# Where operands begin in SBUF: pools of an attention and feed-forward kernel laid out by role

## The chip, the cores and the metric

The kernel runs on one core of a Trainium2 chip. The metric is the device time of one execution in microseconds (us), the median of the runs shown. Matrix products run on TensorE (PE, with its weight loads as PEld), elementwise work on VectorE (DVE) and ScalarE (ACT), and transfers are issued by SyncE (SP) and GpSimd (POOL).

## The reference

Chunked local attention feeds a two-layer network with a PReLU between the layers. Cut to what matters:

```python
# q, k, v: (8, 8, 576, 64); chunks of 64
scores = scale * q_c @ k_c.T               # per chunk
attn = softmax(scores)
out = attn @ v_c
x = out.transpose(0, 2, 1, 3).reshape(4608, 512)
h = x @ w_in                               # (4608, 512) @ (512, 2048)
g = maximum(h, 0) + alpha * minimum(h, 0)
return g @ w_out                           # (4608, 2048) @ (2048, 512)
```

## The kernel before

The 4608 tokens are 9 blocks of 512 (`TB`). Blocks 0 to 2 are computed plainly ("plain blocks"). Blocks 3 to 8 are taken as three pairs with a fast scheme of seven products instead of eight for 2x2 blocks of each layer (`first_product`, `second_product`). Every float32 operand of the feed-forward part is held as two float32r halves, high and low, and each product is three passes: high by high, high by low, low by high.

All feed-forward matmuls have one shape. The weights (`lhsT`, the stationary operand) are 128x128, the moving operand (`rhs`) is 128x512, and the moving operand is read through `woven`, which goes over a 2048-byte row in four rounds: in each it takes 16 bytes of every 64 bytes in turn. There are 16 chunks `f` of the hidden dimension. In a plain block and chunk, `first_layer` has 12 matmuls with weights from `wi[f]` and the moving operand `xh` or `xl`; `ffn_out` has 12 with weights from the activations `gh`, `gl` and the moving operand `wo[f]`. In a pair, weights are units of 128x2x2x256 that `stream` brings back from DRAM into a ring of four tiles (twice the name "raw", and the rooms of `wi15` and `wo15`); `weight` hands out a half of a unit and, when a unit is used up, drops it and issues the next transfer. The moving operands of a pair's first layer are the seven combinations `ops[i, k]` made by `convert`, which lie in rooms of weight chunks that are dead by then (`rooms`); those of its second layer are made by `operand` in small buffers ("gh", "gl", "g", "ta", "tb", "more", "ob"). The activations `g[f]` of a pair lie in rooms of weight chunks too.

Buffers come from pools. A pool has one place for each name (or `bufs` places), and pools lie behind one another in SBUF in the order in which they are opened. Before the change every `wi`, `wo` chunk and everything put into their rooms is in the one pool `const`. In the kernel before, the whole of `const`, `load`, `soft`, `xp`, `gp` and `stage` has places whose byte address is a multiple of 512, since `small`, ahead of them, ends at byte 5120 and every place is 2048, 4096 or 8192 bytes long; in all the feed-forward matmuls, weights and moving operand both begin at a multiple of 512 bytes.

The order of the start is written out by hand in `START`. After it the order of instructions on an engine comes from a scheduler with priorities, except that PE's matmuls keep program order from step 20 on. Of the steps, PE is fed by `prepare` (splitting weights on DVE and ACT, line 189 writes the low half), by `prelu` and the split behind it (lines 386, 389, 415, 418), and in pairs by lines 703 to 720 and 644, 645. Between steps, `visit` does the attention of later tokens (lines 252 and 368).

Of the kernel before, what the change touches and what calls it, by code (L numbers as in the profile page):

```python
# [59 lines left out]
def tile_local_attention_prelu_ffn(  # L60
# [13 lines left out]
    P = 128  # L74
# [18 lines left out]


    small = ctx.enter_context(tc.tile_pool(name="small", bufs=1))
    const = ctx.enter_context(tc.tile_pool(name="const", bufs=1))
    load = ctx.enter_context(tc.tile_pool(name="load", bufs=1))
    soft = ctx.enter_context(tc.tile_pool(name="soft", bufs=1))
    xp = ctx.enter_context(tc.tile_pool(name="xp", bufs=2))
    gp = ctx.enter_context(tc.tile_pool(name="gp", bufs=2))  # L100
    stage = ctx.enter_context(tc.tile_pool(name="stage", bufs=2))
    dram = ctx.enter_context(tc.tile_pool(name="dram", bufs=1, space=bass.MemoryType.DRAM))
# [12 lines left out]

    def room(n, shape, dtype=F32):
        side, f = ("wi", NF - 1 - n // 2) if n % 2 else ("wo", NF - 1 - n // 2)
        return const.tile(shape, dtype, name=f"{side}{f}")  # L120

    FREE = 12
    RAWS = 6
# [5 lines left out]
    nc.scalar.activation(table, table, AF.Exp)  # L129

    small.tile([P, 24], F32, name="rest")
    ident = small.tile([P, P], F32, name="ident")
    make_identity(nc, ident)
    alpha_sb = small.tile([P, NF], F32, name="alpha_sb")
# [14 lines left out]
    def fetch(side, f):  # L149
        n = fetched[0]  # L150
        fetched[0] += 1
        at = n % (4 + RAWS)
        if n < LISTED and at >= 4:
            raws[side, f] = room(FREE + at - 4, [P, 512], I64)
        else:
            name = ("raw", "raw", "more", "more")[at] if n < LISTED else ("raw", "raw", "more")[(n - 14) % 3]
            raws[side, f] = stage.tile([P, 512], I64, name=name, bufs=2)
        latest[0] = nc.sync.dma_start(out=raws[side, f], in_=(w_in if side == "wi" else w_out)[:, f])

    def piece(side, f, alone=False):  # L160

        raw = raws.pop((side, f))
        words = raw.bitcast(U32).rearrange("p (n two) -> p two n", two=2)
        low, high = words[:, 0], words[:, 1]
        name = HALVES.get(f"{side}{f}", halves_free[0])
        halves_free.remove(name)
        t1 = stage.tile([P, 512], U32, name=name, bufs=1)
        w = const.tile([P, 2, 512], F32R, name=f"{side}{f}")
        (wi if side == "wi" else wo)[f] = w
        hi, lo = w[:, 0], w[:, 1]  # L170
        if alone:
            nc.vector.tensor_scalar(t1, high, 0x7FFFFFFF, None, op0=ALU.bitwise_and)
        else:
            nc.scalar.activation(f32(t1), f32(high), AF.Abs)
        yield
        nc.vector.tensor_scalar(f32(t1), f32(t1), bits(0x38000000), bits(0x47EFFFFF), op0=ALU.max, op1=ALU.min)
        yield
        nc.vector.tensor_scalar(t1, t1, 3, 0x3FFFFFF8, op0=ALU.logical_shift_left, op1=ALU.bitwise_and)
        yield
        nc.vector.scalar_tensor_tensor(t1, in0=high, scalar=0xC0000000, in1=t1, op0=ALU.bitwise_and, op1=ALU.bitwise_or)  # L180
        yield
        nc.vector.scalar_tensor_tensor(t1, in0=low, scalar=29, in1=t1, op0=ALU.logical_shift_right, op1=ALU.bitwise_or)
        yield
        if alone:
            nc.vector.tensor_copy(hi, f32(t1))
        else:
            nc.scalar.copy(hi, f32(t1))
        yield
        split_ends[side, f] = nc.vector.tensor_tensor(lo, f32(t1), f32(hi), op=ALU.subtract)
        halves_free.append(name)  # L190
        yield
# [254 lines left out]
    def store(acc, b, keep, tiles=range(SPB)):  # L446
        for t in tiles:
            o = acc[t]
            rows = slice(b * TB + t * P, b * TB + (t + 1) * P)
            before = partial.get((b, t))  # L450
            if b == PLAIN - 1:
                ob = const.tile([P, DM], F32, name=f"wi{NF - 2 - t}")
            elif keep and b == 0:
                side = "wi" if t % 2 else "wo"
                ob = const.tile([P, DM], F32, name=f"{side}{NF - 1 - t // 2}")
            elif keep:
                pool, name = ((load, "q_sb"), (load, "v_sb"), (load, "v_sb"), (soft, "pr"))[t]
                ob = pool.tile([P, DM], F32, name=name, bufs=1 if name == "pr" else 2)
            elif t < 2:
                if t == 0:  # L460
                    both = stage.tile([P, 2, DM], F32, name="more", bufs=2)
                ob = both[:, t]
            elif t == 2:
                ob = stage.tile([P, DM], F32, name="ob", bufs=1)
            else:
                ob = gp.tile([P, DM], F32, name="g")
            with tc.high_priority(offset=HIGH):
                if b == 1 and t > 1 and not keep:
                    nc.vector.tensor_copy(ob, o)
                else:  # L470
                    nc.scalar.copy(ob, o)  # L471
            if keep:
                partial[b, t] = dram.tile([P, DM], F32, name=f"partial{b}_{t}")
                nc.sync.dma_start(out=partial[b, t], in_=ob)
            elif before is not None:
                if t < 3:
                    adds.append((before, ob))
                else:
                    nc.gpsimd.dma_start(out=before, in_=ob, accum_op=ALU.add)
                finals.append((out[rows, :], before))  # L480
            else:
                nc.sync.dma_start(out=out[rows, :], in_=ob)
# [94 lines left out]
    def combine(side, j, early):  # L577

        ws = wi if side == "wi" else wo
        pair = [ws[j], ws[JF + j]]  # L580
        left, right = halves
        a = []
        for w, name in zip(pair, ("ta", "tb")):
            t = stage.tile([P, 512], F32, name=name, bufs=1)
            nc.vector.tensor_tensor(t, f32(w[:, 0]), f32(w[:, 1]), op=ALU.add)
            a.append(t)
        a11, a22 = a[0][:, left], a[1][:, right]
        if side == "wi":
            a12, a21 = a[0][:, right], a[1][:, left]
        else:  # L590
            a21, a12 = a[0][:, right], a[1][:, left]
        nc.vector.tensor_tensor(a22, a21, a22, op=ALU.add)
        nc.vector.tensor_tensor(a21, a11, a21, op=ALU.subtract)
        nc.vector.tensor_tensor(a11, a22, a11, op=ALU.subtract)
        nc.vector.tensor_tensor(a12, a12, a11, op=ALU.subtract)
        names = ((2, 4), (3, 1)) if side == "wi" else ((2, 3), (4, 1))
        for t, name in zip(a, names):
            which = ("raw", "raw", "more")[(fetched[0] - 14) % 3] if early else ("raw", "more")[fetched[0] % 2]
            fetched[0] += 1
            w = stage.tile([P, 2, 512], F32R, name=which, bufs=2)  # L600
            nc.scalar.copy(w[:, 0], t)
            nc.vector.tensor_tensor(w[:, 1], t, f32(w[:, 0]), op=ALU.subtract)
            for half, s in zip((left, right), name):
                stored = keep_a(side, {1: 5, 2: 6, 3: 7, 4: 3}[s], j, w[:, :, half])
            if adds:
                to, what = adds.pop(0)
                with tc.issue_after(stored.ins):
                    nc.gpsimd.dma_start(out=to, in_=what, accum_op=ALU.add)
# [7 lines left out]
    def stream():  # L616
        at = loaded[0]
        if at == len(sequence):
            return
        loaded[0] += 1  # L620
        if at % RING < 2:
            t = stage.tile([P, 2, 2, 2 * P], F32R, name="raw")
        else:
            t = const.tile([P, 2, 2, 2 * P], F32R, name=("wi", "wo")[at % RING - 2] + str(NF - 1))
        side, n = sequence[at]
        streamed[0] = nc.gpsimd.dma_start(out=f32(t), in_=units[side][n])  # L626
        ring.append((side, n, t))
# [10 lines left out]
        assert ring[0][:2] == (side, n)  # L638
        return ring[0][2][:, u]

    rooms = [f"{side}{f}" for f in range(NF - 1) for side in ("wi", "wo")]

    def split(t, t_hi, t_lo):
        hi = nc.scalar.copy(t_hi, t)  # L644
# [2 lines left out]
    def convert(b):  # L647
# [4 lines left out]
        def step(i, k, t):  # L652
            if (i, 0) not in ops:
                for kk in range(2):
                    ops[i, kk] = const.tile([P, 2, TB], F32R, name=rooms[2 * ORDERS["wi"].index(i) + kk])
            split(t, ops[i, k][:, 0], ops[i, k][:, 1])

        def difference(i, k):
# [8 lines left out]
                return b12  # L667
            return {1: b11, 3: b22, 2: b21}[i]

        order = [(i, k) for i in (1, 2, 7, 5, 6, 3, 4) for k in range(2)]  # L670
        return ops, [lambda i=i, k=k: step(i, k, difference(i, k)) for i, k in order]

    banks = ["ps_h", "ps_h", "ps_o0", "ps_o1", "ps_o2", "ps_o3"]
# [19 lines left out]
    def first_product(ops, g, j):  # L693
# [16 lines left out]
            nc.vector.tensor_tensor(u, e, u, op=ALU.add)  # L710
            nc.vector.tensor_tensor(t, t, u, op=ALU.add)  # L711
        for n, f in enumerate((j, JF + j)):
            g[f] = const.tile([P, 2, TB], F32, name=rooms[14 + 2 * j + n])
        with tc.high_priority(offset=HIGH):
            prelu(g[JF + j][:, 1], t, JF + j)
        for ps, i, f, col in ((c, 3, j, 1), (d, 4, JF + j, 0)):
# [298 lines left out]
```

## Time and profile before

| what | us |
|---|---|
| median of 3 runs | 789.27 (788.91 to 790.05) |
| the profiled execution's own time | 788.34 |
| its span, first to last instruction | 786.6 |
| PE busy | 776.5 (99%) |
| PEld busy | 641.1 (82%) |
| DVE busy | 651.3 (83%) |
| ACT busy | 451.0 (57%) |
| POOL busy | 185.0 (24%) |

A matmul is shown with its whole passage through the pipeline, 0.38 to 0.40 us, and successive ones overlap, so PE's busy time says only that it had work. What a matmul costs in a row of them is the distance from its start to the next one's start. The chain of waits gives that directly: a piece is a row of matmuls with its length, counted from the start of its first to the start of what follows, and their number. Between two answers of the timeline for one engine, of which one ends later, the difference of lengths over the difference of counts is the same distance.

### The profile page before, as it was taken

Reading aid. Unit: us, or ns where it says so; the run is one execution under the profiler, and the core shown is the slowest. Engines: PE = TensorE matmul, PEld = TensorE weight load, DVE = VectorE, ACT = ScalarE, POOL = GpSimd, SP = SyncE. Lnnn points to the kernel's source line nnn. Section 1 sums busy time; section 2 is a strip of 40 time slices with the busy share of each in tenths; the row PEclk is TensorE's granted clock in tenths of the full one; section 3 lists DMA queues with packets and bytes.
Section 4 is the critical chain, followed back from the end, with each engine's and each line's share of the span. In section 5 each row is a group of like instructions: output and inputs, shape, how many; then the busy total and the mean of one; then the engine's idle time right before and its main releaser. Section 6 shows DMA issues by size and latency. Waiting matters only on the chain.

```text
span 786.6 us, 15439 instructions
## 1 busy us (share of the span) xinstructions
PE 776.5 (99%) x5558; PEld 641.1 (82%) x5558; DVE 651.3 (83%) x1140; ACT 451.0 (57%) x1221; POOL 185.0 (24%) x304
## 2 busy tenths in 40 slices
PE   7999999999999999999999999999999999999998
PEld 6788888888878888888888888888888888888886
DVE  6999989997989986777799797777897976678774
ACT  6975555656667565656657456564574444344542
POOL 1153323442424421111112111111112111221110
PEclk9999999999999999999999999999999999999999
DMA  9769495566969776878865778865556765555574
GB/s 359 313 217 370 179 314 203 201 225 182 275 198 276 244 252 206 284 260 268 273 208 193 241 230 296 263 234 184 198 196 220 240 220 199 198 187 190 200 243 143
DMA packets 69323, 184.53 MB, mean 235 GB/s; under 512 B 10992, under 2 KB 18176, under 8 KB 69120
## 3 DMA queue, kind: packets, MB, share of 16 engines
q0 software_dynamic: 34336, 119.56, 44.5%
q1 hardware_dynamic: 34480, 63.20, 23.3%
q8 instruction: 44, 0.72, 0.4%
q10 hardware_dynamic: 432, 0.79, 0.3%
q14 instruction: 31, 0.25, 0.1%
HBM read 135.27 MB, written 42.99 MB: 227 GB/s over the span
## 4 chain that ended last, share of the span: by engine, by line
PE 94%; ACT 2%; DMA 2%; DVE 1%; SPq 1%; issue 0%; ACTq 0%
PE ps_o L688 19%; PE ps_o L805 19%; PE ps_h L401 16%; PE ps_h L805 10%; PE ps_h L688 9%; PE ps_oa L437 8%; PE ps_ob L437 8%; PE ps_a L368 2%; PE ps_a L252 2%; DMA q_sb<-qT 1%; ACT wo L293 1%; ACT wi L293 1%; SPq L318 1%; DMA pT<-t 0%; PE ps_h L853 0%; DMA k_sb<-kT 0%
## 5 line engine op out<-in xcount | busy, mean ns | idle before, releaser
L401 PE MATMUL ps_h<-xh,wi 128*128 128x512 f32 x384 | 102.9, 388 | 0.2 <-ACT xh L353 0.2
L401 PEld LDWEIGHTS ps_h<-xh,wi 128*128 128x128 f32 x384 | 70.9, 187 | 14.1 <-ACT xh L353 0.4
L267 ACT ACTIVATE pr<-ps_a,mx 128x64 f32<-128x64 f32 x224 | 67.7, 329 | 0.9
L688 PE MATMUL ps_o<-wi,raw 128*128 128x512 f32 x168 | 65.5, 390 | 0.0
L688 PE MATMUL ps_o<-wo,raw 128*128 128x512 f32 x168 | 64.9, 387 | 0.0
L644 ACT CAST gh<-wi 128x512 fp32r<-128x512 f32 x57 | 35.5, 623 | 46.9 <-PE ps_o L805 28.2
L437 PE MATMUL ps_oa<-wo,gh 128*128 128x512 f32 x192 | 58.9, 387 | 0.0
L437 PE MATMUL ps_ob<-wo,gh 128*128 128x512 f32 x192 | 58.7, 386 | 0.0
L401 PE MATMUL ps_h<-xl,wi 128*128 128x512 f32 x192 | 51.3, 385 | 0.0
L267 ACT ACTIVATION_READ_ACCUMULATOR pr<-ps_a,mx 128x1 f32 x224 | 49.3, 220 | 0.0
L415 ACT CAST gh<-g 128x512 fp32r<-128x512 f32 x48 | 30.3, 630 | 33.1 <-DVE g L389 25.5
L645 DVE TENSOR_TENSOR gl<-wi,gh 128x512 fp32r<-128x512 f32 x54 | 37.1, 687 | 10.9 <-ACT gh L644 10.7
L626 POOL DMA_DIRECT2D raw<-wi_a x42 | 22.4, 532 | 100.8 <-PE ps_o L688 55.9
L386 ACT ACTIVATE wo<-gh 128x512 f32<-128x512 f32 x24 | 15.2, 632 | 53.5 <-DVE gh L711 53.5
L626 POOL DMA_DIRECT2D raw<-wo_a x42 | 22.3, 531 | 93.6 <-PE ps_o L805 52.5
L401 PEld LDWEIGHTS ps_h<-xl,wi 128*128 128x128 f32 x192 | 35.9, 187 | 7.3 <-DVE xl L355 0.3
L437 PEld LDWEIGHTS ps_ob<-wo,gh 128*128 128x128 f32 x192 | 36.0, 187 | 6.8
L437 PEld LDWEIGHTS ps_oa<-wo,gh 128*128 128x128 f32 x192 | 35.4, 187 | 7.5 <-ACT more L471 0.3
L389 DVE SCALAR_TENSOR_TENSOR g<-g,rise,ps_h 128x512 f32<-128x512 f32 x48 | 35.6, 741 | 2.3 <-ACT g L386 2.2
L437 PE MATMUL ps_oa<-wo,gl 128*128 128x512 f32 x96 | 37.0, 385 | 0.0
L437 PE MATMUL ps_ob<-wo,gl 128*128 128x512 f32 x96 | 36.9, 385 | 0.0
L688 PEld LDWEIGHTS ps_o<-wi,raw 128*128 128x128 f32 x168 | 31.5, 188 | 6.7
(314 smaller groups left out, 2230.0 us busy)
## 6 DMA issues: line engine op xcount, KB each, us to landing
raw<-wi_a POOLq DMA_DIRECT2D x42, 512.0 KB, 4.6
raw<-wo_a POOLq DMA_DIRECT2D x42, 512.0 KB, 3.5
wi<-wi_a POOLq DMA_DIRECT2D x21, 512.0 KB, 4.1
wo<-wi_a POOLq DMA_DIRECT2D x21, 512.0 KB, 4.2
wi<-wo_a POOLq DMA_DIRECT2D x21, 512.0 KB, 3.5
wo<-wo_a POOLq DMA_DIRECT2D x21, 512.0 KB, 3.6
k_sb<-kT SPq DMA_DIRECT2D x28, 256.0 KB, 4.6
q_sb<-qT SPq DMA_DIRECT2D x28, 256.0 KB, 4.0
```

What stands on the lines that cost most here:

```text
L252: pe(nc.tensor.matmul(att[0][c * C:(c + 1) * C, par, (NP + hp) * C:(NP + hp + 1) * C], lhsT=q_sb[rows, 2 * hp + c], rhs=kb[rows, 2 * hp + ...
L267: last = nc.scalar.activation(pr[:, g], sc3[:, g // NP, g % NP], AF.Exp, bias=mx[:, g], scale=SCALE, accum_out=sm[:, g])
L293: last = nc.scalar.activation(pr[:, g], sc3[:, g % 2, g // 2], AF.Exp, bias=mx[:, g], scale=SCALE, accum_out=sm[:, g])
L389: nc.vector.scalar_tensor_tensor(g, in0=g, scalar=rise[:, f:f + 1], in1=h, op0=ALU.mult, op1=ALU.add)
L401: pe(nc.tensor.matmul(woven(hps), lhsT=wi[f][:, l, k * P:(k + 1) * P], rhs=woven(xx[:, k]), start=(i == 0 and k == 0), stop=(i == 2 and k ...
L415: nc.scalar.copy(gh, g)
L437: pe(nc.tensor.matmul(woven(o), lhsT=a[:, ts], rhs=woven(wo[f][:, l]), start=(f == first and i == 0), stop=(f == last and i == 2),))
L626: streamed[0] = nc.gpsimd.dma_start(out=f32(t), in_=units[side][n])
L644: hi = nc.scalar.copy(t_hi, t)
L645: return hi, nc.vector.tensor_tensor(t_lo, t, f32(t_hi), op=ALU.subtract)
L688: pe(nc.tensor.matmul(woven(ps), lhsT=w[:, l, k * P:(k + 1) * P], rhs=woven(xx[:, xl]), start=first and at == 0, stop=at == n - 1, skip_gr ...
L805: pe(nc.tensor.matmul(woven(ps[m]), lhsT=w[:, l, m * P:(m + 1) * P], rhs=woven(xx), start=i in (1, 5, 2) and j == 0 and n == 0, stop=j == ...
```

## The change

The pool `const` is split, and the pools are opened in the order `small`, `ring`, `wo`, `xp`, `gap`, `wi`, `load`, `soft`, `gp`, `stage`. The name "raw" moves from `stage` into `ring`. The chunk `wo15` is made 128 bytes longer and its weights begin behind these; `wi15` is made 64 bytes longer likewise; both chunks lie first in their pools, so that all other chunks of a pool follow at 128 or 64 bytes modulo 512. A tile of 384 bytes, `between`, fills `gap`. The units of the ring that lie in the rooms of `wi15` and `wo15` begin at the start of the place. The moving operands of a pair's first layer go to `wi0` to `wi13`, in the order in which they are converted; a pair's activations go to `wo0` to `wo13`, `wi14` and `wo14`; the results of plain block 2 are staged in `wo14` to `wo11` instead of `wi14` to `wi11`. No instruction is written anew or left out.

```diff
     small = ctx.enter_context(tc.tile_pool(name="small", bufs=1))
-    const = ctx.enter_context(tc.tile_pool(name="const", bufs=1))
+    ring_pool = ctx.enter_context(tc.tile_pool(name="ring", bufs=2))
+    wo_pool = ctx.enter_context(tc.tile_pool(name="wo", bufs=1))
+    xp = ctx.enter_context(tc.tile_pool(name="xp", bufs=2))
+    gap = ctx.enter_context(tc.tile_pool(name="gap", bufs=1))
+    wi_pool = ctx.enter_context(tc.tile_pool(name="wi", bufs=1))
     load = ctx.enter_context(tc.tile_pool(name="load", bufs=1))
     soft = ctx.enter_context(tc.tile_pool(name="soft", bufs=1))
-    xp = ctx.enter_context(tc.tile_pool(name="xp", bufs=2))
...
+    SHIFT = 16
+    sides = {"wi": (wi_pool, 1), "wo": (wo_pool, 2)}
+
+    def place(name, shape, dtype):
+        return sides[name[:2]][0].tile(shape, dtype, name=name)
+
+    def chunk(side, f):
+
+        pool, shifts = sides[side]
+        n = shifts * SHIFT if f == NF - 1 else 0
+        t = pool.tile([P, n + 2 * 512], F32R, name=f"{side}{f}")
+        return t[:, n:].rearrange("p (l n) -> p l n", l=2)
...
+    def scratch(name, shape, dtype):
+        return (ring_pool if name == "raw" else stage).tile(shape, dtype, name=name, bufs=2)
...
+    gap.tile([P, 6 * SHIFT], F32, name="between")
...
-        w = const.tile([P, 2, 512], F32R, name=f"{side}{f}")
+        w = chunk(side, f)
...
-                ob = const.tile([P, DM], F32, name=f"wi{NF - 2 - t}")
+                ob = place(f"wo{NF - 2 - t}", [P, DM], F32)
...
-            t = stage.tile([P, 2, 2, 2 * P], F32R, name="raw")
+            t = scratch("raw", [P, 2, 2, 2 * P], F32R)
         else:
-            t = const.tile([P, 2, 2, 2 * P], F32R, name=("wi", "wo")[at % RING - 2] + str(NF - 1))
+            t = place(("wi", "wo")[at % RING - 2] + str(NF - 1), [P, 2, 2, 2 * P], F32R)
...
-    rooms = [f"{side}{f}" for f in range(NF - 1) for side in ("wi", "wo")]
+    CONVERTED = (1, 2, 7, 5, 6, 3, 4)
+    rooms = [f"wo{f}" for f in range(NF - 2)] + [f"{side}{NF - 2}" for side in ("wi", "wo")]
...
-                    ops[i, kk] = const.tile([P, 2, TB], F32R, name=rooms[2 * ORDERS["wi"].index(i) + kk])
+                    ops[i, kk] = place(f"wi{2 * CONVERTED.index(i) + kk}", [P, 2, TB], F32R)
...
-            g[f] = const.tile([P, 2, TB], F32, name=rooms[14 + 2 * j + n])
+            g[f] = place(rooms[2 * j + n], [P, 2, TB], F32)
```

## Rows read from the trace of the kernel before

**Rows 1.** Page, busy time: engine, us, share of the span, instructions.

```profile
PE 776.5 (99%) x5558; PEld 641.1 (82%) x5558; DVE 651.3 (83%) x1140; ACT 451.0 (57%) x1221; POOL 185.0 (24%) x304
```

**Rows 2.** Waits of PE, the longest: tile and line, engine waited for, us, times, longest.

```profile
PE ps_ob L329 <- ACT wo L293: 1.2, 1, 1.2
PE ps_h L853 <- DVE table L128: 1.1, 1, 1.1
```

**Rows 3.** Chain of waits, in order: start us, length us, engine, tile, line, count.

```profile
76.60 2.68 PE ps_h L401 x12
79.28 1.33 PE ps_oa L437 x6
80.61 1.35 PE ps_ob L437 x6
...
426.06 10.72 PE ps_h L805 x48
436.78 32.15 PE ps_o L805 x144
...
717.59 10.87 PE ps_h L805 x48
728.46 32.66 PE ps_o L805 x144
761.12 10.88 PE ps_h L805 x48
```

**Rows 4.** Windows of lines 401, 437, 688, 805 over the whole span, in this order.

```profile
0.00:786.60 786.60, 139.19 (x576) 106.77 (x576) 1.00 0.69 235
...
0.00:786.60 786.60, 138.19 (x576) 107.33 (x576) 1.00 0.69 235
...
0.00:786.60 786.60, 232.65 (x1008) 187.79 (x1008) 1.00 0.69 235
...
0.00:786.60 786.60, 228.17 (x1008) 188.86 (x1008) 1.00 0.69 235
```

**Rows 5.** PE's timeline around 732 us: start, length, line, out<-in, shape, count.

```profile
731.03 0.38 PE L805 MATMUL ps_o<-gh,raw 128*128 128x512 f32 x1
731.25 0.38 PE L805 MATMUL ps_o<-gl,raw 128*128 128x512 f32 x1
731.48 0.63 PE L805 MATMUL ps_o<-gh,raw 128*128 128x512 f32 x2
731.95 0.39 PE L805 MATMUL ps_o<-gl,raw 128*128 128x512 f32 x1
```

**Rows 6.** PEld's timeline: two loads after a stall, then the same place as above.

```profile
150.35 0.30 PEld L401 LDWEIGHTS ps_h<-xh,wi 128*128 128x128 f32 x2
...
731.03 0.19 PEld L805 LDWEIGHTS ps_o<-gl,raw 128*128 128x128 f32 x1
731.26 0.41 PEld L805 LDWEIGHTS ps_o<-gh,raw 128*128 128x128 f32 x2
```

**Rows 7.** PE's timeline at the start, to 2.5 us and to 4 us.

```profile
1.06 1.86 PE L853 MATMUL ps_h<-wo 128*128 128x128 f32 x7 [1.06 <-DVE table L128]
...
1.06 3.35 PE L853 MATMUL ps_h<-wo 128*128 128x128 f32 x14 [1.06 <-DVE table L128]
```

**Rows 8.** Windows: us, PE, PEld, DVE, ACT, POOL busy (x), PEclk, DMA, GB/s.

```profile
40.00:60.00 20.00, 20.00 (x120) 16.55 (x119) 19.97 (x38) 14.54 (x26) 11.13 (x15) 1.00 0.66 234
60.00:80.00 20.00, 20.00 (x91) 16.75 (x90) 19.49 (x38) 11.47 (x20) 6.80 (x9) 1.00 0.97 368
80.00:100.00 20.00, 20.00 (x91) 16.77 (x90) 18.71 (x35) 11.37 (x20) 5.43 (x8) 1.00 0.47 167
100.00:120.00 20.00, 20.00 (x92) 16.75 (x91) 17.32 (x33) 10.89 (x20) 5.54 (x8) 1.00 0.93 329
```

**Rows 9.** DVE's timeline (split of `wi8`) and PE's timeline (its first use).

```profile
83.75 0.69 DVE L189 TENSOR_TENSOR wi<-tb,wi 128x512 fp32r<-128x512 f32 x1 [0.35 <-ACT wi L187]
...
87.16 0.83 PE L401 MATMUL ps_h<-xh,wi 128*128 128x512 f32 x3
```

**Rows 10.** DMA issues of the ring: count, KB, median us to landing.

```profile
raw<-wi_a POOLq DMA_DIRECT2D x42, 512.0 KB, 4.6
wo<-wi_a POOLq DMA_DIRECT2D x21, 512.0 KB, 4.2
```

**Rows 11.** Costliest DVE group in the pairs: busy us, mean ns, idle before.

```profile
L645 DVE TENSOR_TENSOR gl<-wi,gh 128x512 fp32r<-128x512 f32 x54 | 37.1, 687 | 10.9 <-ACT gh L644 10.7
```

**Rows 12.** Chain of waits between first and second product of the first pair.

```profile
397.35 0.60 DVE gl L645
397.95 0.26 DVE wi L741
398.21 0.27 issue
398.48 0.69 DVE tb L645
399.17 0.04 issue
399.21 26.85 PE ps_o L805 x119
```

More of the change, by code (lines that the diff above doesn't have):

```diff
@@ L113, in woven @@
         return t.rearrange("p (a n c) -> p n a c", n=4, c=4)
+    SHIFT = 16
[7 more added lines that the diff above has]
+        return t[:, n:].rearrange("p (l n) -> p l n", l=2)
     def room(n, shape, dtype=F32):
-        side, f = ("wi", NF - 1 - n // 2) if n % 2 else ("wo", NF - 1 - n // 2)
-        return const.tile(shape, dtype, name=f"{side}{f}")
+        f = NF - 1 - n // 2
+        return place(f"wi{f}" if n % 2 else f"wo{f}", shape, dtype)
+    def scratch(name, shape, dtype):
+        return (ring_pool if name == "raw" else stage).tile(shape, dtype, name=name, bufs=2)
     FREE = 12
@@ L156, in fetch @@
             name = ("raw", "raw", "more", "more")[at] if n < LISTED else ("raw", "raw", "more")[(n - 14) % 3]
-            raws[side, f] = stage.tile([P, 512], I64, name=name, bufs=2)
+            raws[side, f] = scratch(name, [P, 512], I64)
         latest[0] = nc.sync.dma_start(out=raws[side, f], in_=(w_in if side == "wi" else w_out)[:, f])
@@ L451, in store @@
             if b == PLAIN - 1:
-                ob = const.tile([P, DM], F32, name=f"wi{NF - 2 - t}")
+                ob = place(f"wo{NF - 2 - t}", [P, DM], F32)
             elif keep and b == 0:
                 side = "wi" if t % 2 else "wo"
-                ob = const.tile([P, DM], F32, name=f"{side}{NF - 1 - t // 2}")
+                ob = place(f"{side}{NF - 1 - t // 2}", [P, DM], F32)
             elif keep:
@@ L599, in combine @@
             fetched[0] += 1
-            w = stage.tile([P, 2, 512], F32R, name=which, bufs=2)
+            w = scratch(which, [P, 2, 512], F32R)
             nc.scalar.copy(w[:, 0], t)
@@ L668, in difference @@
             return {1: b11, 3: b22, 2: b21}[i]
-        order = [(i, k) for i in (1, 2, 7, 5, 6, 3, 4) for k in range(2)]
+        order = [(i, k) for i in CONVERTED for k in range(2)]
         return ops, [lambda i=i, k=k: step(i, k, difference(i, k)) for i, k in order]
```

## The prediction

> **What bounds the kernel now.** I read the page's busy times first. PE has work for 99% of the span, the next engine for 83% [rows 1]. That alone does not say that PE runs at its rate, so the waits of PE come second: the longest are 1.2 and 1.1 us, once each, both in the hand-written start [rows 2]. From 40 us to the end, almost nothing but PE's own pace and the short stalls around an attention visit counts. Third comes the chain of waits, which gives that pace: pieces of 24 matmuls in 2.68 + 1.33 + 1.35 = 5.36 us and pieces of 48 and 144 in 10.72 and 32.15 us are 223.3 ns from start to start; later pieces of 48 and 144 in 10.88 and 32.66 us are 226.7 ns [rows 3]. There are two paces and nothing between: 223.3 ns holds from 40 to 276 us (but for one step) and from 398 to 469 us, 226.7 ns in the rest. The feed-forward matmuls are 576 + 576 + 1008 + 1008 = 3168 [rows 4]; some 75 of them are followed by a stall, and of the other 3095 about 1250 go at the shorter pace and 1850 at the longer, a mean of 225.3 ns. They are 3095 x 0.2253 = 697 us of the 786.6.
>
> What could such a matmul cost at best? The granted clock is 1.00 in every window, so PE is at its upper level of 2.4 GHz [rows 8]. The warm-up matmuls of line 853 give a floor: seven more of them take 3.35 - 1.86 = 1.49 us, 213 ns each [rows 7]. I estimate the same for 512 columns at a column a cycle: 512 / 2.4 = 213.3 ns. So a feed-forward matmul pays 10.0 or 13.3 ns above the floor, 12.0 in the mean, 37 us altogether. It is not paid to another engine: DVE is busy 19.97 us of 20 at 40 us and 17.32 at 100 us, the DMA share goes from 0.47 to 0.97, and PE keeps the pace [rows 8, 3]. What runs beside every one of them is the next matmul's weight load: the matmul at 731.25 us and the load for its successor both start within 0.01 us, again at 731.48 [rows 5, 6]. Single spacings there are 0.22, 0.23 and, for two together, 0.47 us [rows 5]: a recurring pattern, as if what is lost depended on how the two reads of SBUF stand to each other. All of them begin at a multiple of 512 bytes.
>
> The sizes fit reads that meet, though that is arithmetic and no proof. One weight row is 512 bytes, eight blocks of 64. Two loads after a stall follow each other by 0.30 - 0.19 = 0.11 us [rows 6], some 13 ns a block. The moving read takes 16 bytes (four columns, 1.67 ns) of each block in turn and so goes round 512 bytes in 13.3 ns too. Six meetings of 1.67 ns are 10.0 ns, eight are 13.3 ns: just the two paces.
>
> **The change part by part.** *Where operands begin.* `small` ends at byte 5120, `ring` adds 2 x 4096, so `wo` starts at 13312, a multiple of 512; its chunks lie at 128 modulo 512 behind the longer `wo15`, and so do `xh`, `xl`. The gap of 384 bytes brings `wi` back to 0, its chunks to 64, and `load`, `soft`, `gp`, `stage` to 64. Then: plain first layer, weights 64 and moving 128; plain second layer, weights `gh`, `gl` 64 and moving `wo` 128; pairs, weights in the ring 0 and moving operands in `wi0` to `wi13`, `gp` or `stage` 64. Every matmul's moving operand is 64 bytes on from its own weights and from those loaded beside it. So the change does reach all 3168, in all stages.
>
> *What that is worth.* No feed-forward matmul of the trace has another relation than 0, so the price is bounded by rows. The best end is the floor, 213.3 ns: 12.0 x 3095 = 37 us less. The other end is above zero: spacings of 0.24 us would be 0.0147 x 3095 = 45 us more. (0.24 is two together at 0.47 rounded up, the longest the rows suggest.) One row speaks against any gain: the warm-up has weights and moving operand in the same tile, so also at the same place modulo 512, and loses nothing [rows 7]; but it reads its columns in plain order, not in sixteens, so it meets its weight read differently. I take 218 ns, near the shortest spacing that the present relation shows by itself, 0.22 us [rows 5], about 60% of the excess gone: 7.3 x 3095 = 22.6 us less.
>
> *The rule that weighs here.* The Trainium skill ("TensorE: Matmul & The Clock Gate", section "What happens when you issue a matmul") says that PE reads weights and moving operand through two independent ports, so that loading weights takes nothing from a running matmul. By that rule the change would be worth nothing, 789 us; it stands as the second rival below. The same page gives 215.7 ns between warm matmuls of 512 columns; the trace disagrees with 223.3 and 226.7, and by that figure a loss of 9.6 ns could go, 29.7 us and 759.5 us, as an estimate.
>
> *What keeps up with a faster PE.* DVE is the closest. Between 40 and 120 us it works 19.97 + 19.49 + 18.71 + 17.32 = 75.5 us of 80 [rows 8]; PE's 80 us would become 80 x 218 / 223.3 = 78.1, so DVE still fits. The tightest weights there are `wi8`: split done at 83.75 + 0.69 = 84.44, first used at 87.16 us, 2.7 us of cover [rows 9]. PE will be 5.3 / 223.3 x 47 = 1.1 us ahead by then, 2.1 us at the floor. No wait, cost 0; without that cover it would be what PE is ahead. In the pairs, PE reaches the second product of the first pair only after a chain of DVE (0.27 us of waiting, then line 645) [rows 12]: the 65 matmuls just before it may win nothing, 0.5 us. The ring holds four units of 12 matmuls, so a transfer has 36 matmuls, 7.8 us at 218 ns, against 4.6 us to landing [rows 10]. Writing a unit 64 bytes off a multiple of 512 has no row (the ring itself stays at 0); chunks and combinations are written by ACT and DVE, whose operations now begin at 64 or 128. I take no change; if each DVE operation of 687 ns [rows 11] took 5% more, the first 20 us of rows 8 would be overfull by 1 us, and later stages hide it.
>
> *Rooms that move.* The last combination is put in `wi12`, `wi13` at step 15 of block 2, and `wi13` is last read at step 13, two steps of 5.36 us earlier. The results of block 2 go to `wo14`, last read a step earlier. A pair's `wo10`, `wo11` are written five `j` later, some 50 us. None waits; before, the rooms were free still earlier, so the cover is 5 us where a miss would cost at most that once. DMAs, their queue (POOL for the ring, SP for results) and their number stay.
>
> *Sum.* 788.34 - 22.6 + 0.5 = 766.2 us for an execution like the profiled one, 786.6 of it span and 1.7 around it. The median of the runs lies 0.9 us over the profiled one: 767 us.
>
> **The rivals.** *Same:* the excess is PE's own or comes at any shift, since a moving read that goes round all eight blocks meets a weight read that sits in one of them once a round wherever it begins. For it: the sizes above, and that 0 shift has both 10.0 and 13.3. Against it: nothing but the stand of the two reads can make two stable paces with one shape of matmul. 789 us. *Slower:* 64 bytes on, the moving read runs just ahead of the weight read, which steps into each block as the other comes round again; one meeting more than the longer pace, nine of 1.67 ns, is 228.3 ns: 3.0 x 3095 = 9.3 us more, 799 us. It decides from a mean spacing over 225.8 ns. Even settling everywhere on today's longer pace gives 1.4 x 3095 = 4.3 us more, 793.6. For it: which pace a row of matmuls takes is set after a stall, not by the address. *DVE takes part of it back:* PE gets to 218 ns but waits in the plain blocks after 40 us for weights or the split, whose DVE stage is nearly full [rows 8]; the 520 matmuls from 40 to 160 us then win nothing, 3.8 us, 771 us. Against it: 2.7 us of cover.
>
> **How the numbers follow.** The forecast has 0.61, the same 0.12, slower 0.19, DVE 0.08. Under 0.2% (1.6 us) a change can't be told from none here; that is 0.5 ns a matmul. Faster is the forecast and DVE's case, 0.69; same 0.12; slower 0.19. The likeliest one's own range is 757 to 784 us, spacings from 215 to 223.6 ns. For 8 times in 10 the range must take in the same and the milder slower cases: 757 to 794 us leaves out some 0.06 below, towards the floor, and 0.12 above.
>
> **What would show it.** Right: pieces of 48 in the chain at about 10.5 us instead of 10.72 and 10.88, at one pace or several, in plain blocks and pairs alike; the same few waits of PE; DVE's durations as they were. Wrong: pieces still at 10.72 and 10.88 (the addresses do not matter), or above 10.88 (the meeting has got worse), or gains in the pairs alone with PE waiting on DVE after 40 us.

## The result, and the profile after

The changed kernel takes 780.93 us (779.54 to 783.24, four runs) beside 789.09 of the kernel before: a ratio of 0.9899 [0.9873, 0.9926], 8 us less. The forecast was 767: right in sign and in the thing that moves, too large by more than half.

The page after, busy times as in [rows 1]:

```profile
span 779.4 us, 15439 instructions
PE 767.0 (98%) x5558; PEld 641.4 (82%) x5558; DVE 650.9 (84%) x1140; ACT 449.8 (58%) x1221; POOL 185.2 (24%) x304
```

The instructions are the same in number, and the other engines' busy times are within 1.2 us of what they were. The profiled execution took 781.14 us, 7.2 less than the one before, and its span is 7.2 shorter.

The chain of waits after (start us, length us, engine, tile, line, count), the pieces that answer to [rows 3]:

```profile
76.18 2.68 PE ps_h L421 x12
...
426.91 10.69 PE ps_h L826 x48
...
712.25 10.56 PE ps_h L826 x48
722.81 31.68 PE ps_o L826 x144
```

Three things are to be seen. In the plain blocks nothing has moved up to the visit at 139 us: 12 matmuls in 2.68 us, 223.3 ns, as before. At 427 us the pieces of 48 have gone from 10.72 to 10.69, 222.7 ns, and the piece there starts 0.85 us later than before, while the one at 76 us started 0.4 earlier: up to here more has been given away than won, and the whole net gain comes after it. In the last pairs they have gone from 10.87 to 10.56, and 144 from 32.66 to 31.68: 220.0 ns. That pace holds from 545 us on; between 139 and 545 us the stretches between stalls mostly run into 220.0, 222.7 or 223.3 ns, and which one changes from stretch to stretch. PE's timeline in the last pairs (start, length, line, out<-in, shape, count) shows the starts a constant 0.22 us apart, without the 0.23 of [rows 5]:

```profile
701.53 0.38 PE L826 MATMUL ps_o<-ta,raw 128*128 128x512 f32 x1
701.75 0.38 PE L826 MATMUL ps_o<-tb,raw 128*128 128x512 f32 x1
701.97 0.60 PE L826 MATMUL ps_o<-ta,raw 128*128 128x512 f32 x2
```

For all stages I took from each trace the distances from start to start of successive feed-forward matmuls, those under 300 ns, and divided them by order into five stretches, the first to about 146 us, the next to 319, 477 and 625 us and the end. Mean ns, with the kernels of the experiments below:

```
                       to 146   to 319   to 477   to 625  to end    all
before                  223.4    224.3    224.9    226.6   226.7   225.25
changed                 223.4    222.9    222.5    221.1   220.0   221.89
changed, run again      223.3    222.4    222.8    222.8   222.7   222.76
shift0                  223.5    224.2    226.5    226.3   226.7   225.53
shift32                 225.0    223.2    222.8    225.4   225.3   224.31
shift128                225.7    229.3    229.6    229.6   230.0   229.00
ring208                 222.9    222.0    220.2    220.4   220.0   221.01
```

The waits of PE from 41 us to the end (tile and line, engine waited for, us, times, longest), of the changed kernel and then of the kernel before:

```profile
PE ps_o L826 <- DVE tb L666: 0.8, 1, 0.8
PE ps_a L388 <- ACT xl L399: 0.8, 2, 0.4
PE ps_a L388 <- PE ps_h L421: 0.6, 1, 0.6
PE ps_oa L457 <- ACT more L491: 0.3, 1, 0.3
PE ps_o L709 <- ACT gh L724: 0.2, 1, 0.2
PE ps_a L388 <- DMA pT<-t: 0.2, 1, 0.2
```

```profile
PE ps_a L368 <- DMA pT<-t: 0.4, 1, 0.4
```

So 2.9 us of waits stand where 0.4 stood. The longest is the gap that [rows 12] lead to. In the changed kernel's chain DVE is late there (first fence), and PE's timeline shows the hole (second fence; the bracket is the wait, with what ended it):

```profile
399.42 0.69 DVE tb L666
400.11 0.04 issue
400.16 26.76 PE ps_o L826 x119
```

```profile
398.97 0.38 PE L826 MATMUL ps_o<-ta,wi 128*128 128x512 f32 x1
400.16 0.49 PE L826 MATMUL ps_o<-tb,wi 128*128 128x512 f32 x1 [0.81 <-DVE tb L666]
```

The start here is 1.19 us after the one ahead of it, where it was 0.52:

```profile
398.69 0.39 PE L805 MATMUL ps_o<-ta,wi 128*128 128x512 f32 x1
399.21 0.49 PE L805 MATMUL ps_o<-tb,wi 128*128 128x512 f32 x1
```

The account from one profiled execution to the other: the distances under 300 ns sum to 685.2 us (3088 of them) after 696.7 (3093), 11.5 less. Of that 3.36 ns x 3088 = 10.4 is pace, and 1.1 are five matmuls that a stall now follows. All other time of PE after 41 us (stalls, attention visits) is 58.0 after 53.3, 4.7 more, or 3.6 without those five matmuls' own. The start and tail are 0.4 shorter: 10.4 - 3.6 + 0.4 = 7.2.

### The profile page after: what moved, and what is told of

The parts are those of the page before. It is cut to its first block, busy times and chain, and to the rows that moved or that the text cites. A ratio compares the mean times of both kernels' runs of the same rounds, so it can differ in the third digit from the quotient of the medians.

```text
span 779.4 us, 15439 instructions
## 1 busy us (share of the span) xinstructions
PE 767.0 (98%) x5558; PEld 641.4 (82%) x5558; DVE 650.9 (84%) x1140; ACT 449.8 (58%) x1221; POOL 185.2 (24%) x304
## 4 chain that ended last, share of the span: by engine, by line
PE 75%; DVE 8%; ACT 7%; DMA 5%; SPq 3%; issue 2%; DVEq 0%; POOL 0%; ACTq 0%
PE ps_o L709 19%; PE ps_o L826 18%; PE ps_h L826 10%; PE ps_h L709 9%; PE ps_h L421 7%; PE ps_oa L457 4%; PE ps_ob L457 4%; SPq L338 3%; ACT pr L287 2%; PE ps_a L388 2%; DMA pT<-t 1%; DMA raw<-w_in 1%; ACT wi L313 1%; DMA raw<-w_out 1%; PE ps_a L272 1%
## 5 line engine op out<-in xcount | busy, mean ns | idle before, releaser
L709 PE MATMUL ps_o<-wi,raw 128*128 128x512 f32 x336 | 79.3, 383 | 0.0
L709 PEld LDWEIGHTS ps_o<-wi,raw 128*128 128x128 f32 x336 | 62.6, 188 | 11.4
L665 ACT CAST gh<-wo 128x512 fp32r<-128x512 f32 x66 | 41.0, 621 | 43.7 <-PE ps_o L826 29.9
L666 DVE TENSOR_TENSOR gl<-wo,gh 128x512 fp32r<-128x512 f32 x63 | 43.2, 686 | 7.6 <-ACT gh L665 7.3
L665 ACT CAST more<-wo 128x512 fp32r<-128x512 f32 x42 | 26.0, 619 | 28.6 <-DVE wo L762 17.5
L709 PE MATMUL ps_o<-wi,wi 128*128 128x512 f32 x168 | 40.7, 384 | 0.2 <-ACT gh L724 0.2
L709 PE MATMUL ps_h<-wi,raw 128*128 128x512 f32 x168 | 40.7, 384 | 0.0
L709 PE MATMUL ps_o<-wi,wo 128*128 128x512 f32 x168 | 40.5, 383 | 0.0
```

Source lines behind the costliest of these rows:

```text
L666: return hi, nc.vector.tensor_tensor(t_lo, t, f32(t_hi), op=ALU.subtract)
L709: pe(nc.tensor.matmul(woven(ps), lhsT=w[:, l, k * P:(k + 1) * P], rhs=woven(xx[:, xl]), start=first and at == 0, stop=at == n - 1, skip_gr ...
```

## Experiments

The theory behind the forecast: what is lost is set by where the moving operand begins against the weights loaded beside it. Rivals: the rooms and the order, which the change moves too, make the gain; or the pace of a row is set by chance after a stall, whatever the address; or the loss is that of reading in sixteens.

**meet1: the dispute by itself.** Rows of 40 matmuls of the kernel's shape and reading order, one stall between rows, four rows a case, with stalls of four lengths.

```diff
+CASES = [(d, 4, 4, 128) for d in (0, 16, 32, 48, 64, 96, 128, 192, 256, 320, 384, 448, 480)]
+CASES += [(0, 1, 512, 128), (64, 1, 512, 128), (256, 1, 512, 128), (0, 4, 4, 64), (0, 4, 4, 32)]
...
+            nc.tensor.matmul(
+                woven(ps[:m], n, c), lhsT=wt[:, k * P:k * P + m], rhs=woven(mv[:, d // 4:d // 4 + 512], n, c),
+                start=i == 0, stop=i == count - 1,
+            )
```

> Not the layer: only rows of 40 matmuls of 512 columns, four rows for each case, each row begun after a wait of another length; the output holds sums of no use. The cases differ in how far the moving operand begins behind its weights modulo 512 bytes (0 to 480), in the order in which columns are read (four rounds of 16 bytes in 64, as in the kernel, or plain), and in the number of weight columns (128, 64, 32). Meeting theory (a matmul's read meets the next one's weight read): spacing changes with the distance; distance 0 shows 223.3 or 226.7 ns, distance 64 shows 220 to 223.3, some distance goes down towards 213 to 216; 64 weight columns pay about half of the 10 to 13 ns, 32 about a quarter. Independent ports theory (the loss is PE's own): every distance and every number of weight columns has the same set of spacings, 220 to 227 ns. Order theory (the loss is of the reading in sixteens): plain order has 213 to 216 ns at every distance.

The chain (columns as above); a piece of 40 is 39 distances and some 0.5 us for slower first ones and the last one's passage, so pieces compare directly. Distance 0 first, 64 from 182.78, 128 at 272.44, 256 at 342.88, 320 from 382.57; 541.34 has distance 0 in plain order; the last two have distance 0 and weights of 64 columns:

```profile
24.70 9.31 PE ps L41 x40
...
54.58 9.23 PE ps L41 x40
...
182.78 9.09 PE ps L41 x40
...
212.09 9.41 PE ps L41 x40
...
272.44 9.85 PE ps L41 x40
...
342.88 9.34 PE ps L41 x40
...
382.57 9.41 PE ps L41 x40
...
541.34 9.38 PE ps L41 x40
...
661.34 8.92 PE ps L41 x40
680.53 9.20 PE ps L41 x40
```

The lasting pace, from the starts in the second half of a row: distance 0 gives 226.7 in three rows and 223.3 in one, the two paces of the kernel before. 64 gives 220.0 twice, 223.3 and 228.4; 128 gives 230 and 240; 256 is as 0, 320 as 64, and 448 and 480 as 192 and (in meet3) 224. 384 agrees with 128 in part: 230 in two rows, but 225.4 in the other two, which no row of 128 had (the kernel shift128 below had it up to 139 us). So the address counts, with a period of 256 bytes, not 512; and one address has several paces. Within a row the pace stays; what picks it at the row's start is not shown. Reading in sixteens is not the loss: plain order gives 226.7 ns at 0 and 256 and 228.7 to 229.1 at 64, in all four rows each, not the 213 to 216 that this rival had. Weights of 64 columns should have halved the meetings; two rows give 216.7 and two 224.3 ns, and with 32 columns 222.8: no proportion to what the load reads. No row ran matmuls without a load beside them.

**shift0: pools, rooms and order of the change, without the distance.**

```diff
-    gap = ctx.enter_context(tc.tile_pool(name="gap", bufs=1))
...
-    SHIFT = 16
+    SHIFT = 0
...
-    gap.tile([P, 6 * SHIFT], F32, name="between")
```

> The changed kernel with its pools and rooms, but with no byte of shift: weights and moving operands at 0 modulo 512 again. If the distance of 64 bytes did it: spacings of 223.3 and 226.7 ns come back, 788 to 790 us, PE pieces of 48 at 10.72 or 10.88 us. If the pools and rooms did it (other waits, other order on DVE and ACT): it stays at 780 to 782 us.

789.86 us, 1.0006 [0.9992, 1.0020]. Its chain, last stretch, and the only wait of PE that the profile lists after 41 us:

```profile
729.42 32.66 PE ps_o L824 x144
```

```profile
PE ps_a L386 <- ACT xl L397: 0.3, 1, 0.3
```

That is [rows 3] again, and of the changed kernel's waits only one on `xl`, shorter. The gain is the distance alone; rooms and order cost nothing on the whole. Two visits, at 254 and 275 us, do take 0.3 to 0.4 us longer than before here too, and one at 222 us takes 0.3 less, so a part of what these two grow by in the changed kernel is not due to the distance.

**meet2: does the distance count, or the place? And the order of reading.**

```diff
+CASES = [(64, 64, 4, 4, 128), (64, 128, 4, 4, 128), (128, 192, 4, 4, 128)]
+CASES += [(0, d, 4, 4, 128) for d in (8, 24, 40, 56, 72, 80)]
+CASES += [(0, 0, n, c, 128) for n, c in ((2, 4), (8, 4), (16, 4), (32, 4), (2, 8), (4, 8), (8, 8), (4, 16), (8, 2))]
...
```

> Again only rows of matmuls (32 in a row, four rows for each case, begun after waits of four lengths); the output holds sums of no use. First cases: weights and moving operand both at 64, or at 64 and 128, or at 128 and 192 modulo 512. If the distance between the two counts: the paces of distance 0 (223.3, 226.7 ns) for the first, those of 64 (220, 223.3, 228.4) for the others. If the place of the moving operand alone counts: 64 behaves as distance 64, and 128 as distance 128 (230, 240). Then distances that are no multiple of 16 bytes: if a 16-byte piece is the unit, they cost more than their neighbours, since a piece then lies in two; if not, they lie between. Then other orders of reading (2, 8, 16, 32 rounds; pieces of 8, 32 and 64 bytes) at distance 0 and 64: the meeting theory has paces that change with the order; independent ports have 220 to 227 ns throughout.

The chain, pieces of 32: weights and moving both at 64, then 64 and 128 (two rows), then 0 and 8:

```profile
24.73 7.52 PE ps L43 x32
...
65.38 7.33 PE ps L43 x32
73.36 7.43 PE ps L43 x32
...
121.16 14.60 PE ps L43 x32
```

Both moved by 64 is as both at 0 (226.7 ns over whole cycles); 64 apart from another place is as 64 from 0. The distance counts. A moving operand 8, 24, 40, 56 or 72 bytes on takes 446 to 456 ns, twice the time; every multiple of 16 that was tried in the same order stayed at 240 or below. That is not the clock: it fell to 0.5 for 3.4 us in most of these rows, but those with a granted clock of 1.00 throughout took 446.7 to 453.3 ns all the same. No other order of reading beat the kernel's at distance 0 on the whole: two rounds 231 to 233 ns, eight 247, sixteen 276 to 279, thirty-two 268; four rounds of 32 bytes had 220 ns in one row and 230.7 in three.

**shift128 and shift32: more and less distance in the kernel.**

```diff
-    SHIFT = 16
+    SHIFT = 32
...
-    gap.tile([P, 6 * SHIFT], F32, name="between")
+    gap.tile([P, 64], F32, name="between")
```

> The changed kernel with 128 bytes in place of 64 between weights and moving operands, in every stage. The rows of matmuls alone had 230 and 240 ns at this distance, and 225.4 at its double period 384. If the distance sets the pace in the kernel too: 230 ns in most stretches, up to 240 in some, so 3095 x (4.7 to 14.7) ns more than at distance 0: 803 to 835 us, slower than the kernel before by 2% or more. If any distance but 0 helps: 780 us, as with 64.

799.24 us, 1.0127 [1.0100, 1.0154]: slower, by less than the 803 to 835 expected. Its last stretch:

```profile
737.08 33.12 PE ps_o L826 x144
```

144 in 33.12 us are 230.0 ns, the lower of meet1's paces for 128; 240 came nowhere to stay. And PE's other time shrank to 50.6 us: a slower PE waits less.

shift32 is the same with `SHIFT = 8` and 112 for 64.

> The changed kernel with 32 bytes in place of 64. The rows alone had two paces, 220.0 and 225.4 ns, half of the rows each. If the distance sets the paces and the state after a stall chooses: stretches at one or the other, a mean near 222.7, 779 to 784 us, and from run to run up to 1048 x 5.4 ns = 5.7 us apart, as the last stretch goes. If only whole blocks of 64 bytes count: as at distance 0, 789 us.

787.48 us, 0.9980 [0.9966, 0.9994], where 779 to 784 was expected. meet1 had 220.0 and 225.4 ns for 32 bytes. From 477 us on, the kernel ran at the second:

```profile
728.28 32.45 PE ps_o L826 x144
```

A distance is worth the pace that its stretches take, not the best pace that it can have.

**nudge: the changed kernel with four small matmuls more in the last attention visit**, so that the stall ahead of the last stretch differs and the addresses don't.

```diff
-        for hp in range(NP):
+        for hp in (*range(NP), *([NP - 1] if s == NSUB - 1 else [])):
```

> The changed kernel, with the last four small matmuls of the last attention visit made twice (same operands, same values), so that the last stretch of some 1050 matmuls without a stall begins some 58 ns later than it would. If the state at the start of a stretch chooses its pace: the last stretch, at 220.0 ns in the changed kernel, goes at another pace of distance 64 (222.7, 223.3 or 228.4 ns), 3 to 9 us more by that alone. If the pace belongs to the operands: 220.0 ns again and the time as it was.

781.6 us in a single run. The last 1048 matmuls go at 222.7 ns, not 220.0:

```profile
722.64 32.06 PE ps_o L826 x144
```

That is not to be put down to the added matmuls: stretches well ahead of them differ from the first profile too (the one at 139 us for one), and the next run has the same 222.7 without them.

**again: the changed kernel, unaltered,** to see what its runs differ by.

> The changed kernel itself once more, unaltered, on the same chip. If the state after a stall chooses the pace: stretches of the plain blocks and the pairs at other paces of distance 64 than in the first profile, though each at 220.0, 222.7, 223.3 or 228.4 ns, and single times some us apart, 779 to 784 us. If the first profile's paces belong to the program: the same pace stretch by stretch.

783.11 us (779.80 to 783.73), 0.9914 [0.9898, 0.9929]. Its last stretch in the profiled run:

```profile
724.21 32.07 PE ps_o L826 x144
```

So the same program takes 220.0 in one execution and 222.7 in another. The first long stretch, 430 matmuls from 41 us, went at 223.3 ns in both and in nudge. Over 1048 matmuls that is 2.8 us, two thirds of the spread of its ten single times, 779.5 to 783.7 us.

**meet3: the distances left out so far, in search of one with a single low pace.**

```diff
+CASES = [(0, d, 4, 4, 128) for d in (112, 144, 160, 176, 208, 224, 240, 64, 64, 32, 32)]
...
```

> Rows of matmuls alone once more (32 in a row, four rows each), output of no use: the distances of whole 16-byte pieces below 256 that were not tried (112 to 240), 64 and 32 twice, fewer weight columns at 64 and 128, and pieces of 32 bytes at other distances. If paces repeat every 256 bytes and every pace is a multiple of some step of 6.67 ns over a few matmuls: the new distances fall on such values, 220 to 240 ns, and 224 repeats the 226.7 of 480. If some distance lets the reads pass each other wholly: 213 to 217 ns there in all four rows, 8 to 12 ns below distance 0, and it is the one to build. With 32 weight columns: if the weights' own read is what is met, distance does not matter any more and the loss is near 3 ns; if not, 222 to 223 ns as before at distance 0.

The chain; two of the four rows of 208 bytes:

```profile
153.16 7.36 PE ps L41 x32
...
161.24 7.35 PE ps L41 x32
```

208 alone has 220.0 ns in all four rows. 144 has 220.0 and 222.2, 112 has 222.2 in all four, 160 has 225.7, 176 has 223.3 and 226.3, 224 has 226.7, 240 has 230 to 230.9. No row came to the 213 to 217 hoped for. With 32 weight columns distance still matters: 221.7 at 64, and at 128 three rows of 216.7 and one of 230.2.

**ring208: 208 modulo 256 in the pairs (weights at 16, moving operand at 224), 64 in the plain blocks.**

```diff
-    SHIFT = 16
-    sides = {"wi": (wi_pool, 1), "wo": (wo_pool, 2)}
+    SHIFT = 8
+    sides = {"wi": (wi_pool, 7), "wo": (wo_pool, 1)}
...
-    gap.tile([P, 6 * SHIFT], F32, name="between")
+    gap.tile([P, 7 * SHIFT], F32, name="between")
...
-            t = scratch("raw", [P, 2, 2, 2 * P], F32R)
+            t = scratch("raw", [P, 1024 + 64], F32R)
...
+        t = t[:, 4:4 + 1024].rearrange("p (u l n) -> p u l n", u=2, l=2)
```

> The changed kernel with the pairs' 2016 matmuls at a distance of 208 bytes modulo 256 (weights in the ring at 16, moving operands at 224) and the plain blocks' 1152 at 64 as before. In the rows alone 208 was the one distance at which all four rows ran into 220.0 ns and stayed. If the distance sets which paces there are and the state after a stall chooses among them: every stretch of the pairs at 220.0 ns after a few matmuls, plain blocks at 220 to 225 as in the changed kernel, 777 to 780 us, and no spread from the last stretch. Rival, that the kernel's last stretch was only lucky: the pairs at several paces as with 64, 781 us or more.

780.41 us (779.52 to 780.70), 0.9884 [0.9869, 0.9899], just above the 777 to 780 expected; on the same chip the changed kernel had the 783.11 above. There it is a little faster and steadier; against the changed kernel's first four runs (780.93) the difference is within the intervals. Its chain from the middle on, where the kernel before needed 10.87 and 10.88 and the changed kernel had 220.0 ns in one execution and 222.7 in another:

```profile
553.43 10.56 PE ps_h L827 x48
...
722.39 31.68 PE ps_o L827 x144
```

The pairs are at 220.0 ns but for a few short stretches (means 220.0 to 220.4), and the distances sum to 680.5 us, 4.7 less than in the changed kernel's profile. Yet the span, 778.9, is only 0.5 less: the other time is 61.7 us after 58.0, and the start and tail are 0.5 longer. Its longest waits of PE:

```profile
PE ps_o L827 <- DVE tb L667: 0.9, 1, 0.9
PE ps_a L388 <- PE ps_h L421: 0.6, 1, 0.6
```

**ringpool and ringgp: ring208 with something taken off the busy queues**, to win that time back. ringpool gives the weight combinations' additions to POOL:

```diff
-            nc.vector.tensor_tensor(t, f32(w[:, 0]), f32(w[:, 1]), op=ALU.add)
+            nc.gpsimd.tensor_tensor(t, f32(w[:, 0]), f32(w[:, 1]), op=ALU.add)
```

> The kernel with 208 bytes in the pairs, and besides, in combine, the two sums of a weight's halves (two DVE operations of 0.69 us in each of 16 steps between 107 and 233 us) are made on POOL instead. If the new stalls of PE between 160 and 280 us and at 389 and 399 us come from DVE being late for a faster PE: PE's time outside the rows of matmuls after 41 us, 61.7 us in the kernel with 208 bytes and 53.3 in the kernel before, falls back towards 57, 774 to 778 us. If they come from other links of that chain (SP's issues and landings of the transposed probabilities, ACT's exponentials), or POOL is slower at the sums and DVE then waits for it: 780 us or more.

819.88 us, 1.0383 [1.0361, 1.0404]. The first fence is a group of those additions (busy us, mean ns, idle before), the second PE's longest wait:

```profile
L605 POOL TENSOR_TENSOR ta<-wi 128x512 f32<-128x512 f32 x8 | 11.9, 1490 | 0.1
```

```profile
PE ps_oa L457 <- ACT more L491: 18.2, 2, 12.1
```

An addition takes 1.39 to 1.49 us on POOL, against 0.69 for DVE's of that size [rows 11], and PE waits for the attention work behind it. That is not the whole cost: the granted clock was 0.5 in five stretches between 178 and 340 us, 31 us together, where ring208 had 1.00; one window of it, with the columns of [rows 8]:

```profile
186.00:199.00 13.00, 3.84 (x9) 3.07 (x10) 5.81 (x12) 5.70 (x23) 9.23 (x11) 0.50 0.70 205
```

How much of the 39 us more the waits cost and how much the clock is not shown. ringgp issues half of the transfers of `pT` from POOL:

```diff
-                    nc.sync.dma_start(
+                    (nc.gpsimd if c else nc.sync).dma_start(
```

> The kernel with 208 bytes in the pairs, and besides, four of the eight transfers that turn a visit's probabilities (pT) are issued from POOL's queue instead of SP's. In the changed kernel's chain between 170 and 290 us the eight issues follow each other at 0.6 to 1.4 us, then 3.4 us to landing, then PE. If this chain is what PE has become bound by: PE's time outside the rows of matmuls after 41 us falls from 61.7 us towards 57, 775 to 778 us. If DVE and ACT ahead of it are late anyway, or POOL's queue is held by transfers that wait: 780 us or more.

785.35 us, 0.9941 [0.9926, 0.9955], slower than ring208 with PE waiting for ACT again:

```profile
PE ps_oa L457 <- ACT more L491: 2.8, 2, 1.7
PE ps_a L388 <- ACT xl L399: 2.5, 2, 2.0
```

Both failed as tests: they made PE wait elsewhere. What would give the lost time back stays open.

**shift256: the period, in the kernel.** `SHIFT = 64` and no gap.

> The changed kernel with 256 bytes between weights and moving operands in every stage. If what counts repeats every 256 bytes, as the rows of matmuls alone showed: the paces of distance 0, 223.3 and 226.7 ns, 788 to 790 us. If it repeats every 512 bytes, as the change has it: paces of their own, another time.

789.84 us, 1.0008 [0.9994, 1.0023]: 256 bytes apart is as good as none.

```profile
568.71 10.88 PE ps_o L824 x48
```

## Why the prediction was right and where it was wrong

*What bounds the kernel now* held: PE's pace sets the time, and the pace moves with the addresses. *Where operands begin* held, with a period of 256 for 512: "64 bytes on" is right, "modulo 512" is not (256 and 320 go as 0 and 64).

*What that is worth* failed, as the largest term of the sum: 22.6 us predicted, 10.4 measured. I took 218 ns for every matmul, the mean is 221.9: 28% of the 12.0 ns above the floor went, not 60%. I had picked 218 from single spacings of 0.22 in the old pattern, but these steps are part of a cycle. In the kernel before, a cycle of 218, 230, 224 and 221 ns makes up the 223.3, and [rows 5] lie in a stretch at 226.7, a cycle of seven steps from 220 to 239 ns; the shortest step does not hold by itself. The nearest pace that lasts is 220.0, and it held only from 545 us on, before that in some short stretches; the 501 matmuls to 146 us stayed at 223.4. At 220.0 everywhere the term would have been 5.25 x 3088 = 16.2 us. That the profiled execution had 220.0 at its end was luck: run again, it had 222.7 there.

The floor was misread as well. [rows 7] show the warm-up matmul at 213 ns before 5 us; from 7.4 us on the same matmul goes at 112, as here twelve in 1.50 us, the last one's passage of 0.28 with them:

```profile
11.42 1.50 PE L853 MATMUL ps_h<-wo 128*128 128x128 f32 x12
```

The record of the granted clock begins only at 6.7 us, and these matmuls have 128 columns. So [rows 7] say nothing of 512 columns at the upper clock, and that they come to 213.3 like the estimate is chance. Nor does the plain order explain them: 512 columns in plain order took 226.7 ns (meet1). No row came below 216.7.

Beneath it lies a second fault, the picture of six and eight meetings of 1.67 ns. Half the weight columns don't halve the loss, and a quarter loses more than two of the rows with half. Many lasting paces are near simple multiples of 6.67 ns (220.0 is 33 times, 223.3 is 33.5, 226.7 is 34, 230 is 34.5, 240 is 36), but 222.7, 225.4 and 228.4 are not. What is met, and why 208 has one pace, stays open.

*What keeps up with a faster PE* failed as well, as a term: 0.5 us predicted, 3.6 measured. The place I named, the first pair's second product, took 0.67 us more (a wait of 0.81), near the 0.5 that I had put there. `wi8` and the split did keep up, as said, and so did the ring's transfers. What I put at nothing are the attention visits, where PE now waits for ACT, for `pT`'s transfer and for its own result. In the chain after, such a visit (two of its issues on SP are shown):

```profile
173.79 0.72 DVE t L331
...
177.63 1.15 SPq L338
...
178.82 0.59 SPq L338
...
179.46 3.36 DMA pT<-t
```

From transpose to landing 9.0 us pass on DVE, SP and the DMA, none of which gets faster with PE. That the waits come in the main with PE's pace and not from the rooms is shown by the kernels with the same rooms: other time 50.6 us at 229.0 ns (shift128), 53.6 at 225.5 (shift0), 55.5 at 224.3 (shift32), 58.0 at 221.9 (changed), 61.7 at 221.0 (ring208). From shift0 to the changed kernel 3.6 ns, 11 us of pace, gave 4.4 us back, of which 1.3 is only the ordinary time of six more matmuls that a stall now follows. The next 0.9 ns, 2.7 us, gave 3.7 back, of which 2.0 is that of nine more.

*Rooms that move* held on the whole: shift0 is at 1.0006 with an interval that holds 1.

*The rivals.* "Same" falls with shift0 against the changed kernel: one program but for the distance, 789.9 and 780.9 us. So does the rule of the Trainium skill ("TensorE: Matmul & The Clock Gate", section "What happens when you issue a matmul") that loading weights takes nothing from a running matmul: 128 bytes apart costs 230.0 ns and 64 apart 220.0. Whether the two reads share a port is not shown. The 215.7 ns of that page was not reached as a lasting pace by any row; the lowest with 128 weight columns is 220.0. "Slower" came at another distance, 128; it was right that in these runs a pace changes only after a stall, though the address sets which paces there are, and that keeps the gain apart from the best pace. "DVE takes part of it back" had the right direction and the wrong place: the feed-forward matmuls of the plain blocks wait 0.3 us for ACT (`ps_oa`) and not for DVE, and they did not win pace up to 146 us either; the wait for DVE is in the first pair.

Of the signs I had named, "about 10.5" for pieces of 48 came true at the end (10.56), not "in plain blocks and pairs alike"; "the same few waits of PE" did not.

## What to carry to other kernels

Where weights are loaded beside every matmul, read the distance from start to start from long pieces of the chain, and try where the moving operand begins against its weights in short rows by themselves, several rows a case: one row shows one pace of several, and a single step of a cycle is no pace. Prefer the distance whose rows all agree (208 modulo 256 here) to one whose best row is the best. Then price what a faster engine will meet next from the visits that run at other engines' times: here 35% of what the pace had won was gone again.

## What the runs showed of the hardware that was not expected

- The period is 256 bytes, and only the distance counts: 256 goes as 0 (226.7 ns), 320 as 64 (220.0 to 228.3), 384 as 128 in part, weights and moving operand both moved by 64 as neither (226.7).
- One address has several lasting paces (64 bytes: 220.0, 222.7, 223.3, 228.4 ns). After the first matmuls behind a stall a stretch keeps its pace, 1048 matmuls long at most here, and the same program takes different ones in different executions (220.0 and 222.7 ns in the last stretch). What picks it stays open.
- Moving operands that begin 8 bytes off a multiple of 16 took 446 to 456 ns for 512 columns, twice the time, at a granted clock of 1.00.
- With 128 weight columns no distance lasted below 220.0 ns; with 64 columns two rows of four ran at 216.7 at distance 0, with 32 columns three of four at distance 128.
